# Two output banks taken in turn through the tail, and the second layer's weights loaded and cast every fifth slot

## The chip, the core and the metric

The kernel runs on one core of a Trainium2 chip. A core has five engines that run beside each other, each through its own instructions in order: TensorE (PE in the profile; its weight loads are listed as PEld), VectorE (DVE), ScalarE (ACT), GpSimd (POOL) and SyncE (SP), which here only issues DMA transfers. Engines wait for each other through semaphores. TensorE writes to PSUM, a memory of eight banks; VectorE and ScalarE read results from there and write them to SBUF, the working memory.

The metric is the device time of one execution in microseconds (us), shown as the median of several runs.

## The reference

An attention whose weights below a threshold are dropped, and then a two-layer network on its output. q, k and v have 8 batches of 8 heads, 576 rows and 64 columns; `x` has 4608 rows and 512 columns, `w_in` is 512 x 2048, `w_out` is 2048 x 512.

```python
scores = scale * np.matmul(q, k.transpose(0, 1, 3, 2))
thresh = np.max(scores, axis=-1, keepdims=True) - tau
scores = np.where(scores >= thresh, scores, -1000000000.0)
scores = scores - np.max(scores, axis=-1, keepdims=True)
attn = np.exp(scores)
attn = attn / (np.sum(attn, axis=-1, keepdims=True) + 1e-09)
attn_out = np.matmul(attn, v)
...
x = attn_out.transpose(0, 2, 1, 3).reshape(B * S, H * D)
h = x @ w_in
g = h - np.tanh(h)
out = g @ w_out
```

## The kernel before

**Attention.** Two heads form a pair (32 pairs, four to a batch), and a pair's 1152 rows of queries form nine tiles of 128, so there are 288 tiles. The main loop (line 681) has one slot `s` for each tile and some more on both ends. In slot `s` it issues the scores of tile `s + 8` (`scores`, lines 310 and 320, into two PSUM buffers `psS`), the thresholding of a tile some slots back (`kink`, line 367, ScalarE), the exp of tile `s` (`weights`) and the product with v of tile `s - 2` (`attend`, lines 422 and 433, into the PSUM tile `psO` of the pool `ps_o`, which has one buffer). `norm` (lines 447 to 453) takes `psO` out, and `emit_x` (lines 465 to 479) turns a pair's result and files it as `xT` and `xR`. VectorE takes each tile's scores out of PSUM with the row maximum (line 330).

**How z is turned.** For the first six pairs (tiles 0 to 53) TensorE transposes the thresholded tile z (line 387). From tile 54 on SyncE issues a DMA transpose for it (line 375), two tiles at a time or one alone, and ScalarE's exp of line 404 reads the result `zT`.

**Preparing a pair.** `plan` sets it out by tiles ahead of need. SyncE loads k, q and v (lines 149 to 157) some 14 to 16 tiles ahead into two buffers each. GpSimd splits k and q into a high and a low half (lines 183 to 187), later copies the turned k with its halves swapped (`kS`, line 263) and casts v (lines 215 to 220). For pair p, with r the tile whose scores the slot issues, the split of k stands at r = 9p - 8, the split of q at 9p - 7, the turn of k with its `kS` at 9p - 5, the cast of v at 9p - 4. The loads for it stand at 9p - 16 to 9p - 14.

**The weights.** `w_in` and `w_out` come in eight pieces each of 512 KB (128 x 1024 in f32). At every r in the list `w_when` (line 664) GpSimd casts the piece loaded at the event before (`w_cast`, line 618) and SyncE issues the load of the next (`w_load`, lines 626 and 630). The pool `wt` has two buffers, so a load waits for the cast of two pieces earlier. With the list of before the first eight events load `w_in`, the ninth (r = 35) casts the last piece of it and loads the first of `w_out`, and the seventeenth (r = 67) casts the last piece.

**The network.** It runs in nine blocks m: eight of 512 rows, one for each batch, and a ninth that gathers the 64 rows left over in each. `hidden` (line 488) makes one of sixteen columns of h from four matmuls of 512 columns; ScalarE's tanh (line 501, `bend`) and VectorE's subtraction (line 507, `shrink`) make g. `project` (line 514) makes a quarter of a group: for 128 rows (`ms` = 0 to 3) it adds four of the sixteen chunks of g times `w_out` into one PSUM tile `psY`; at the last quarter the tile is copied to the SBUF tile `yo` (lines 522 or 524; two buffers) and a store is put on SyncE's queue. A group is called (m, ms) below.

`layers(m, tail)` lists the steps of one stage: the sixteen `h_step` of block m, and between them the `y_step` of block m - 1 that are still to do, from its fourth quarter on. Stages 0 to 6 are spread over the slots of the attention (from slot 40 on), with the tail flag off. Stages 7 and 8 come after the last tile, with the flag on: first (6, 0)'s last quarter, (6, 1) to (6, 3), the first three quarters of (7, 0), then the rest of (7, 0), (7, 1) to (7, 3) and three groups of block 8. The last group is done in two halves of 256 columns (`y_half`).

**The banks of the tail.** `psY` comes from `ps_y`, which has one buffer. In the tail attention is done with `ps_o`, and a group may take that one; its copy is then made by ScalarE (line 522) and not by VectorE (line 524). Line 558 sets which: odd `ms` from block 7 on. So (6, 1), (6, 2), (6, 3) and (7, 0) follow each other on `ps_y`, and then (7, 1), (7, 3) and (8, 1) lie on `ps_o`. The first half of the last group takes `ps_o` and the second `ps_y`; ScalarE copies the first half, VectorE the second. In the tail h takes `psH` (two buffers) and `psHt` (the two buffers of the scores) in turn.

Of the kernel before, what the change touches and what calls it, by code (L numbers as in the profile page):

```python
# [18 lines left out]
def kernel(  # L19
# [14 lines left out]
    B, H, S, D = q.shape  # L34
# [96 lines left out]
    ps_o = pool("ps_o", 1, space=PSUM)  # L131
    ps_h = pool("ps_h", 2, space=PSUM)
    ps_y = pool("ps_y", 1, space=PSUM)
# [350 lines left out]
    def hidden(m, n, ps):  # L484
        if n == 0:
            gs[m] = g_pool.tile([P, DF_C, MB], BF16, name="g")
        for c in range(DM_C):
            nc.tensor.matmul(  # L488
                out=ps, lhsT=w_in_sb[:, c, n * P : (n + 1) * P],
                rhs=xs[m][:, c, :] if m < B else xR[:, c, :, :],  # L490
                start=(c == 0), stop=(c == DM_C - 1),
            )
        halves.append((m, n, ps))
# [18 lines left out]
    def project(m, ms, part, ps, last, cols=slice(0, d_model)):  # L512
        for n in range(4 * part, 4 * part + 4):
            nc.tensor.matmul(  # L514
                out=ps, lhsT=gs[m][:, n, ms * P : (ms + 1) * P],
                rhs=w_out_sb[:, n, cols], start=(n == 0), stop=(n == DF_C - 1),
            )
        if part == 3:
            nc_ = cols.stop - cols.start
            yo = y_pool.tile([P, nc_], F32, name="yo")  # L520
            if last:
                nc.scalar.copy(out=yo, in_=ps)
            else:
                nc.vector.tensor_copy(out=yo, in_=ps)  # L524
            if m < B:
                rows = out[m * S : m * S + MB, :].rearrange("(p c) n -> c p n", c=4)
                stores.append(lambda: nc.sync.dma_start(out=rows[ms], in_=yo))
            else:
                for h in range(2):
                    b = 2 * ms + h  # L530
                    eng = nc.scalar if h and nc_ < d_model else nc.sync
                    stores.append(
                        lambda b=b, h=h, eng=eng: eng.dma_start(
                            out=out[b * S + MB : (b + 1) * S, cols],
                            in_=yo[64 * h : 64 * h + 64, :],
                        )
                    )
# [8 lines left out]
    def layers(m, tail):  # L546


        def h_step(n):
            if tail and n % 2:  # L550
                ps = ps_big.tile([P, MB], F32, name="psHt", tag="big")
            else:
                ps = ps_h.tile([P, MB], F32, name="psH", tag="h")
            hidden(m, n, ps)

        def y_step(m, ms, part):
            if part == 0:
                odd = ms % 2
                odd = odd and m >= B - 1
                pl, tag = (ps_o, "o") if tail and odd else (ps_y, "y")  # L560
                ys[m, ms] = pl.tile([P, d_model], F32, name="psY", tag=tag), odd
            ps, odd = ys[m, ms]
            project(m, ms, part, ps, tail and odd)

        def y_half(h):

            n = d_model // 2
            pl, tag = ((ps_y, "y"), (ps_o, "o"))[1 - h]
            ps = pl.tile([P, n], F32, name="psY", tag=tag)
            for part in range(4):  # L570
                project(m, 3, part, ps, h == 0, slice(h * n, h * n + n))

        now = quarters(m - 1)[EARLY(m - 1) :] if m > 0 else []
        if m < NMB - 1:
            now += quarters(m)[: EARLY(m)]
        else:
            now += quarters(m)[:12]
        n = 16 + len(now)


        ahead = n - max(0, EARLY(m) - 3) - LAST if m < NMB - 1 else n - 9 - LAST
        steps, at, i = [], [], 0

        def ready(y):
            last = 4 * y[2] + 3
            return y[0] < m or len(at) > (last if m else 15) and at[last] + 2 < i

        while now or len(at) < 16:
            if len(at) < 16 and (
                not now or not ready(now[0]) or len(at) * ahead <= i * 16  # L590
            ) and not (m == B - 1 and i < FIRST):
                steps.append(lambda a=len(at): h_step(a))
                at.append(i)
            elif ready(now[0]):
                steps.append(lambda y=now.pop(0): y_step(*y))
            else:
                steps.append(lambda: None)
            i += 1
        if m == NMB - 1:
            steps += [lambda h=h: y_half(h) for h in range(2)]  # L600
        return steps
# [4 lines left out]
    def w_pieces():  # L606
        for w, sb, n in ((moe_w_in, w_in_sb, DM_C), (moe_w_out, w_out_sb, DF_C)):
            flat = sb.rearrange("p c n -> p (c n)")
            cols = n * w.shape[1] // 8
            src = w.rearrange("(c p) n -> p c n", p=P)  # L610
            for i in range(8):
                yield flat, src, i, cols, w.shape[1]
# [48 lines left out]
    for t in ("k", "q", "v"):  # L661
        load(1, t)
    pieces = w_pieces()
    w_when = [4 * i + 3 for i in range(17)]

    todo, stage = [], 0
    fold = const.tile([P, 64], BF16, name="fold")
# [122 lines left out]
```

## Time and profile before

| | |
|---|---|
| median of 7 runs | 539.14 us (538.36 to 540.0) |
| the profiled execution | 537.61 us |
| its span, first to last instruction | 535.8 us |
| granted TensorE clock | 0.999 |
| busy: TensorE, VectorE, ScalarE, GpSimd | 509.8, 428.1, 436.8, 290.1 us |
| first `psY` matmul | 113.1 us |
| last attention product (`psO`) | 465.2 us |
| first and last cast of `w_out` | 59.9 and 104.5 us |
| copies `yo`: VectorE, ScalarE | 33 and 4 |

The page divides the span into 40 slices and gives each engine's busy share of a slice in tenths. The groups say how often a line ran, how long one took, and what ended the engine's idle time before it. The chain of waits is followed back from the last instruction: each entry has its start, its length and the engine and line that worked; "issue" is time in which nothing that the profile shows was waited for. The timeline lists instructions with start and length, and in brackets the idle time of the engine just before. A DMA has the time at which it was issued and the time from there to its landing. The ends of matmuls are modelled.

### The profile page before, as it was taken

The numbers are of one execution on the slowest core, as the hardware profiler recorded it, in microseconds if no ns is written. First come the engines' busy times: TensorE is split into PE (matmuls) and PEld (weight loads), VectorE is DVE, ScalarE is ACT, GpSimd is POOL, SyncE is SP. The second block draws the span as 40 slices with busy tenths as digits, with TensorE's granted clock in tenths as the row PEclk, the third lists the DMA queues.
The fourth block names the chain that finished last, engine by engine and source line by source line (L and its number), as shares of the span: only waits on it lengthen the run. The fifth ranks groups of instructions, "written<-read, shape, count | busy, mean of one in ns | idle before, by whom it ended". The sixth has DMA issues, their size and how long they took to land.

```text
span 535.8 us, 13026 instructions
## 1 busy us (share of the span) xinstructions
PE 509.8 (95%) x4771; PEld 287.1 (54%) x4771; DVE 428.1 (80%) x1203; ACT 436.8 (82%) x628; POOL 290.1 (54%) x390
## 2 busy tenths in 40 slices
PE   5999899999999999999999999999999999999997
PEld 3666565555555555555555555555455555444444
DVE  5988888989888989888888988898888887554440
ACT  5999888999898989899888989898989989533330
POOL 7999996767555756666655755575666620000000
PEclk9999999999999999999999999999999999999999
DMA  7554657899988998899989899899989976300113
GB/s 215 170 185 150 206 177 145 187 189 180 197 178 160 183 206 182 168 174 188 197 175 198 182 195 189 161 176 203 186 164 175 204 135 116 88 30 30 39 41 78
DMA packets 204768, 85.76 MB, mean 160 GB/s; under 512 B 172320, under 2 KB 197152, under 8 KB 204704
## 3 DMA queue, kind: packets, MB, share of 16 engines
q1 hardware_dynamic: 204112, 84.51, 74.1%
q8 instruction: 37, 0.61, 0.5%
q10 hardware_dynamic: 592, 0.43, 0.3%
q14 instruction: 27, 0.22, 0.1%
HBM read 36.70 MB, written 9.44 MB: 86 GB/s over the span
## 4 chain that ended last, share of the span: by engine, by line
PE 70%; DVE 17%; ACT 4%; POOL 4%; issue 2%; DMA 1%; ACTq 0%; DVEq 0%; SPq 0%; POOLq 0%
PE psY L514 20%; PE psH L488 18%; PE psS L320 15%; DVE sc L330 8%; PE psO L433 5%; PE psS L310 3%; DVE g L507 3%; PE ps_k L234 3%; PE psHt L488 2%; ACT pT L396 2%; DVE kT L257 2%; DVE yo L524 2%; ACT z L367 1%; PE ps_q L234 1%; PE psZ L387 1%
## 5 line engine op out<-in xcount | busy, mean ns | idle before, releaser
L330 DVE TENSOR_SCALAR_CACHE_REDUCE sc<-psS 128x576 f32<-128x576 f32 x288 | 216.0, 752 | 23.3 <-PE psS L320 13.4
L367 ACT ACTIVATE z<-sc,nb 128x576 bf16<-128x576 f32 x256 | 193.4, 768 | 19.1 <-DVE nb L347 19.1
L514 PE MATMUL psY<-w_out_sb,g 128*128 128x512 bf16 (+1 forms) x592 | 146.0, 374 | 1.6 <-DVE yo L524 1.6
L263 POOL COPY kS<-kT 64x1152 f16<-64x1152 f16 x62 | 70.7, 1141 | 128.4 <-DVE nb L347 126.8
L404 ACT ACTIVATE pT<-zT 128x1152 f16<-128x1152 bf16 (+1 forms) x130 | 138.8, 1068 | 0.7 <-PE psX L471 0.5
L488 PE MATMUL psH<-xT,w_in_sb 128*128 128x512 bf16 x480 | 124.0, 379 | 2.3 <-DVE g L507 2.3
L320 PE MATMUL psS<-kT,qT 128*128 128x512 f16 (+1 forms) x512 | 104.9, 286 | 6.9 <-DVE sc L330 3.9
L501 ACT ACTIVATE th<-psH 128x512 f32<-128x512 f32 x128 | 75.4, 589 | 37.9 <-PE psH L488 36.7
L320 PEld LDWEIGHTS <-qT 128*128 128x128 f16 x1024 | 72.6, 97 | 56.5 <-issue 9.7
L507 DVE SCALAR_TENSOR_TENSOR g<-th,psH 128x512 bf16<-128x512 f32 x128 | 87.3, 682 | 18.9 <-ACT th L501 18.9
L320 PE MATMUL psS<-kS,qT 128*128 128x512 f16 x496 | 101.3, 286 | 0.3 <-POOL kS L263 0.3
L514 PEld LDWEIGHTS <-g 128*128 128x128 bf16 x592 | 50.7, 98 | 58.2 <-issue 5.7
L488 PEld LDWEIGHTS <-w_in_sb 128*128 128x128 bf16 x576 | 49.2, 98 | 58.2 <-issue 4.5
L433 PEld LDWEIGHTS <-pT 128*128 128x128 f16 x1280 | 55.7, 98 | 25.3 <-issue 1.9
L433 PE MATMUL psO<-vb,pT 128*128 128x65 bf16 x1280 | 61.2, 193 | 0.0
L187 POOL TENSOR_TENSOR qhl<-qraw,qhl 128x576 f16<-128x576 f32 x31 | 39.7, 1280 | 2.6
L187 POOL TENSOR_TENSOR khl<-kraw,khl 128x576 f16<-128x576 f32 x31 | 39.7, 1279 | 2.7
L396 ACT ACTIVATE pT<-psZ 128x640 f16<-128x640 bf16 (+1 forms) x54 | 35.4, 658 | 5.2 <-PE psZ L387 4.9
L257 DVE COPY kT<-ps_k 128x1152 f16<-128x1152 f16 x31 | 23.4, 756 | 13.8 <-PE ps_k L234 13.8
L524 DVE COPY yo<-psY 128x512 f32<-128x512 f32 (+1 forms) x33 | 22.5, 682 | 12.7 <-PE psY L514 7.6
L448 DVE TENSOR_TENSOR osb<-psO,rc 128x256 bf16<-128x256 f32 x64 | 27.2, 424 | 2.2
L234 PE MATMUL ps_k<-ident_f,khl 128*128 128x128 f16 x288 | 21.7, 220 | 5.3 <-DVE khl L200 5.2
(78 smaller groups left out, 504.9 us busy)
## 6 DMA issues: line engine op xcount, KB each, us to landing
vraw<-in_v_dram SPq DMA_DIRECT2D x32, 256.0 KB, 3.4
out_dram<-yo SPq DMA_DIRECT2D x32, 256.0 KB, 2.8
kraw<-in_k_dram SPq DMA_DIRECT2D x31, 256.0 KB, 3.2
qraw<-in_q_dram SPq DMA_DIRECT2D x31, 256.0 KB, 3.7
wt<-in_moe_w_in_dram SPq DMA_DIRECT2D x8, 512.0 KB, 4.6
wt<-in_moe_w_out_dram SPq DMA_DIRECT2D x8, 512.0 KB, 4.1
zT<-z SPq DMA_TRANSPOSE x104, 3.5
kraw<-in_k_dram SPq DMA_DIRECT2D x32, 32.0 KB, 3.0
```

The lines of the kernel that those rows point to most:

```text
L187: nc.gpsimd.tensor_tensor(out=hl[:, :, 1, :], in0=x, in1=hl[:, :, 0, :], op=ALU.subtract)
L263: nc.gpsimd.tensor_copy(out=o, in_=i)
L320: nc.tensor.matmul(out=ps[:, dst], lhsT=lhs, rhs=kk[:, src], start=(n == 0), stop=(n == 1),)
L330: nc.vector.tensor_scalar(out=sc, in0=ps[:, lo : lo + S], scalar1=SC, scalar2=None, op0=ALU.mult, op1=ALU.max, accum_out=mx[:, c : c + 1],)
L367: nc.scalar.activation(out=z, in_=sc, func=ACT.Prelu, bias=nb, scale=1.0, alpha=STEEP)
L396: nc.scalar.activation(out=pt[:, off * P : (off + n) * P], in_=ps[:, 0 : n * P], func=ACT.Exp)
L404: nc.scalar.activation(out=pt[:, 0 : n * P], in_=zts.pop(i)[:, 0:n, :], func=ACT.Exp)
L433: nc.tensor.matmul(out=po[:, (j - 1 - 5 * hh) + ab, :], lhsT=pt[:, blk * P : (blk + 1) * P], rhs=vb[:, hh, c, :], start=(n == 0), stop=(n ...
L488: nc.tensor.matmul(out=ps, lhsT=w_in_sb[:, c, n * P : (n + 1) * P], rhs=xs[m][:, c, :] if m < B else xR[:, c, :, :], start=(c == 0), stop= ...
L501: nc.scalar.activation(out=th, in_=ps, func=ACT.Tanh)
L507: nc.vector.scalar_tensor_tensor(out=gs[m][:, n, :], in0=th, scalar=-1.0, in1=ps, op0=ALU.mult, op1=ALU.add,)
L514: nc.tensor.matmul(out=ps, lhsT=gs[m][:, n, ms * P : (ms + 1) * P], rhs=w_out_sb[:, n, cols], start=(n == 0), stop=(n == DF_C - 1),)
```

## The change

The first two parts are in the tail. A group takes `ps_o` and ScalarE's copy if the tail flag is on, the group comes after (6, 1), and `ms` is even: (6, 2), (7, 0), (7, 2), (8, 0) and (8, 2). All others take `ps_y` and VectorE's copy. The halves of the last group exchange their banks: the first takes `ps_y`, the second `ps_o`; ScalarE still copies the first and VectorE the second.

The third part is the list of events for the weights. The first nine stay (r = 3, 7, ... 35). The other eight come at r = 40, 45, ... 75 and no longer at 39, 43, ... 67. An event both casts a piece and loads the next, so both move.

```diff
         def y_step(m, ms, part):
             if part == 0:
-                odd = ms % 2
-                odd = odd and m >= B - 1
-                pl, tag = (ps_o, "o") if tail and odd else (ps_y, "y")
+
+                odd = tail and (m, ms) > (B - 2, 1) and ms % 2 == 0
+                pl, tag = (ps_o, "o") if odd else (ps_y, "y")
                 ys[m, ms] = pl.tile([P, d_model], F32, name="psY", tag=tag), odd
             ps, odd = ys[m, ms]
-            project(m, ms, part, ps, tail and odd)
+            project(m, ms, part, ps, odd)
 
         def y_half(h):
 
             n = d_model // 2
-            pl, tag = ((ps_y, "y"), (ps_o, "o"))[1 - h]
+            pl, tag = ((ps_y, "y"), (ps_o, "o"))[h]
             ps = pl.tile([P, n], F32, name="psY", tag=tag)
             for part in range(4):
                 project(m, 3, part, ps, h == 0, slice(h * n, h * n + n))
...
     pieces = w_pieces()
-    w_when = [4 * i + 3 for i in range(17)]
+    w_when = [4 * i + 3 for i in range(9)] + [5 * i + 40 for i in range(8)]
```

## The prediction

> **What bounds the kernel now.** I read the page first (busy shares, slices), then the chain of waits cut to the tail and to its last microseconds, then the timeline of GpSimd and TensorE while the weights are cast, then the DMA issues one at a time where they share the queue with the transposes.
>
> ```profile
> PE 509.8 (95%) x4771; PEld 287.1 (54%) x4771; DVE 428.1 (80%) x1203; ACT 436.8 (82%) x628; POOL 290.1 (54%) x390
> POOL 7999996767555756666655755575666620000000
> ```
>
> TensorE is busy 95% of the span, but stage by stage the picture differs: GpSimd (POOL) is full in slices 2 to 6 (13 to 80 us) and idle after 440 us. The first part of the change sits where TensorE alone counts, the second just where POOL goes from full to half full. The granted clock is 0.999, so it plays no part.
>
> The tail, in the chain of waits (start, us, what):
>
> ```profile
> 470.86 0.88 PE psH L488 x4
> ...
> 472.42 0.57 issue
> 472.99 0.69 DVE yo L524
> 473.69 0.04 issue
> 473.73 1.02 PE psY L514 x4
> 474.75 0.86 PE psH L488 x4
> ...
> 501.54 0.86 PE psHt L488 x4
> 502.40 0.86 PE psY L514 x4
> 503.26 0.86 PE psH L488 x4
> ```
>
> The first six lines are a change of output tile on one PSUM bank: the next psY group can't begin until VectorE has copied the last one out. The last three are such a change with two banks (the ScalarE copy of (7, 1) starts at 501.57): 0.86 after 0.86, no gap. TensorE has no other gap from 466 us to its end, so what is saved there is saved at the end.
>
> The last transfer but one holds the last copy:
>
> ```profile
> 528.41 0.70 DVE yo L524
> 529.11 0.02 issue
> 529.13 0.47 SPq L533
> 529.60 0.05 issue
> 529.65 2.39 DMA out_dram<-yo
> ...
> 532.16 0.42 DVE yo L524
> ```
>
> The last half's copy waits for the buffer yo of (8, 2), whose store lands at 532.04; TensorE's last matmul ends at 531.86 (its merged row: 519.50 + 12.36).
>
> **The tail's banks, costed.** Before, (6,1), (6,2), (6,3) and (7,0) all take ps_y, and alternation begins at (7,1). After, (6,2), (7,0), (7,2), (8,0), (8,2) take ps_o with a ScalarE copy and the odd ones ps_y with VectorE, so three same-bank changes become alternating ones: (6,1) to (6,2), (6,2) to (6,3), (6,3) to (7,0). A step of four matmuls is 0.863 us without a stall (501.54 to 503.26 is two). From psH at 470.86 four steps end at 474.31; the trace has 474.75: 0.44. The same reading at 478.21 to 482.10 and 485.56 to 489.45 gives 0.44 each. **Sum: -1.31.** The change (6,0) to (6,1) stays on one bank (psY at 464.01, an idle of 0.78 before it), since ps_o still holds psO: VectorE reads it at 465.39. By 473.3, when (6,2) wants it, it has been free for some 7 us.
>
> Copies: ScalarE gains five of 0.585 us and loses three, VectorE the reverse at 0.69. They cost nothing, because ScalarE has 1.13 us idle before most tanh rows in the tail and was busy 6.57 of 20 us from 480 to 500; at 501.57 the copy stands directly ahead of a tanh (502.44, idle 0.28), and the matmul steps around it stay at 0.86. Without that cover each of the two added copies would push a tanh by 0.58: at most 1.2 us. The halves swap banks but still alternate: half 0 takes ps_y, left by (8,1) at 525.7 in old times, half 1 takes ps_o, left by (8,2) a full half (1.7 us) earlier. No wait is added. What is late next is the end: (8,2) is now copied in 0.585 instead of 0.69, so its store, and the last copy that waits for it, come 0.10 sooner (bounds 0 and 0.30, where the matmul itself would hold the copy). **Tail: -1.41.**
>
> **The weights' loads and casts, costed.** Nothing changes up to tile 35. The eight w_out pieces, with their loads (512 KB on SP's queue, issue 0.37 to 0.56 us) and casts (1.04 us on POOL), move: casts from tiles 39, 43, ... 67 to 40, 45, ... 75, loads from 35, 39, ... 63 to 35, 40, ... 70. The number of instructions is the same.
>
> On POOL:
>
> ```profile
> 59.87 1.04 POOL L618 CAST w_out_sb<-wt 128x1024 bf16<-128x1024 f32 x1
> 60.97 2.33 POOL L263 COPY kS<-kT 64x1152 f16<-64x1152 f16 x2
> ...
> 63.35 0.41 PE L320 MATMUL psS<-kS,qT 128*128 128x512 f16 x2 [0.29 <-POOL kS L263]
> ```
>
> The cast at 59.87 goes behind the copy kS, which starts at 59.93 (its source kT is there at 58.8), and TensorE's wait of 0.29 disappears. Nearly all of that is swallowed: the next VectorE row on the chain, sc at 63.91, waits for ScalarE's z (63.23 + 0.67), not for these matmuls, whose row ends at 63.76. I take -0.10, bounds 0 and -0.30. The later splits come at most 0.7 to 1.5 us sooner to consumers that don't wait for them (after 83 us POOL idles 2.8 to 5.9 us before every kS). The casts of tiles 70 and 75 fall at about 106 and 112 us into that idle time. First use of the last two pieces is the fourth quarter of (0,0) at about 125 us: cover 11 us. If the cover were gone, each would cost 1.04.
>
> The Trainium skill's page "SBUF — State Buffer", section "Who interferes with whom", speaks against shuffling POOL work under VectorE: an instruction that takes the shared port pair blocks the other engine for its whole length. The trace has 62 kS copies of 1139 to 1144 ns under a VectorE that is 80% busy, so nothing of it shows here; by the rule a moved copy could cost up to one VectorE row, 0.75, by the row 0.
>
> On SP's queue the loads at tiles 55 and later are passed by the transposes zT (issued from 84.86 on). Loads in that stretch: two before (87.74, 95.15), three after (about 90, 99.9 and 108). The one at tile 65 now stands behind the k load (98.68) and ahead of the q load and of this transpose:
>
> ```profile
> 101.20 1.78 SPq L375 DMA_TRANSPOSE zT<-z  x1
> zT<-z SPq DMA_TRANSPOSE x1, 5.5
> 107.61 1.15 ACT L404 ACTIVATE pT<-zT 128x1152 f16<-128x1152 bf16 x1
> ```
>
> (The second line, from the DMA view of 101 to 103 us, is its time to landing.) It lands at 106.7 and the exp takes it at 107.61: slack 0.9. A w load alone takes 3.9 us to land (issued at 76.89) and a 256 KB k load 3.0 (at 98.68), so 256 KB add 0.9 and 512 KB 1.8; less where the queue runs at its best. I take 1.6. The landing becomes 108.3 and ScalarE, gapless from 92 to 118 us, stands 0.7 longer. Behind it wait a tanh (110.00), for it VectorE's g (110.94, slack 0.36) and for that TensorE's psX (111.68): 0.3 of the 0.7 reach TensorE. I take +0.30. Lower bound 0 (the slack holds). Upper bound: the transpose issued at 88.49 right behind a load landed after 6.4, against 3.3 for an undisturbed one, so +3.1, less 0.9 of slack: +2.2. I am nearer the low end, because the k and q loads already delay this transpose (5.5 against 3.3) and the new load only lengthens that line. The load at about 108 is ahead of transposes with slack 3.5 and 3.8 us; removing the one at 87.74 helps rows that had slack 2.1 and 3.1. Both: 0.
>
> The page "DMA: Bandwidth & Descriptors", section "Queues, rings and completion order", says that each DMA engine takes the descriptors of one queue in ring order, which is the rule against putting a bulk load in front of transposes. At that page's 358 GB/s I estimate 1.5 us for 512 KB, and by it the exp would be 0.5 late instead of 0.7.
>
> **Sum.** -1.41 - 0.10 + 0.30 = -1.21. The profiled execution took 537.61 (span 535.8 and 1.81 around it), so 536.4 there. That execution is 1.53 below the median of the seven runs, 539.14 (538.36 to 540.0); a saving at the path's end carries over, so 539.14 - 1.21 = **537.9**, which is -0.22%. What a measurement can tell from no change is about 0.2%, 1.08 us: 538.06 and 540.22 are the marks.
>
> **Rivals.**
> 1. The slots' move is free or a gain: the exp is not late and the 0.29 counts in full. 539.14 - 1.41 - 0.30 = 537.4. For it: only 0.9 us of slack is attacked, by an uncertain queue. Against: ScalarE hides the 0.29. Chance 0.16.
> 2. The tail's gain is partly given back around 107 us: the whole 0.7 of the exp's lateness, or up to twice that, reaches TensorE, undamped, since from 111.68 on TensorE is on the chain. 539.14 - 1.41 + 0.7 = 538.4, with + 1.4 539.1. For it: ScalarE is gapless there. Against: g has slack. Chance 0.20.
> 3. Slower: SP's queue becomes the bound. One mechanism: a load directly ahead of a transpose costs 3.1, as at 88.49, and this happens at the loads of tiles 65 and 70. The first gives 3.1 - 0.9 = 2.2; the second is still unabsorbed at the transposes issued at 114.09 (landed 118.34, used 119.87, slack 1.5), which gives 1.6. 3.8 - 1.41 = +2.4: 541.5. It decides from a total loss of 2.5 us. For it: the transpose issued at 118.61 lands at 122.76 and ScalarE takes it at 122.86 after an idle of 0.51, so slack does reach zero. Against: the DMA digits show empty slices between. Chance 0.12.
> 4. The banks alternate but the wait only changes its name: the copy on ScalarE queues behind a tanh and psY waits as long for it. Tail about 0, total 539.3. The rows at 501.57 and 515.39 speak against it. Chance 0.05.
>
> **Chances.** The forecast has 0.47, with its own range 537.5 to 538.3 (0.39 of it below 538.06). Faster: 0.39 + 0.16 = 0.55. Same: 0.08 + 0.20 + 0.05 = 0.33. Slower 0.12. The range 537.2 to 539.6 takes in rivals 1, 2 and 4 and most of the unknown cost's upper bound (539.14 - 1.41 + 2.2 = 539.9); it leaves out rival 3 and the last of that bound.
>
> **What the new profile would show.** ScalarE's copies yo six (five full ones), VectorE's 31; no psY group behind a VectorE yo wait but the one near 464; steps of 0.86 from there to the end. kS of the fifth pair at about 59.9 and no POOL wait at 63. The sixth transposed exp, near 107.6: its idle time is the price of part two. If the distance from the first psY (113.1) to the old 470.00 psY has changed, something I hold to be steady is not. I am wrong if the start of layer two's first psY moves by more than 1 us, or if the tail from 464 on shortens by less than 1.

## The result, and the profile after

The changed kernel takes 540.43 us (median of 13 runs, 539.35 to 541.29) against 539.14 (median of 31 runs of the kernel before, 538.12 to 541.00). The ratio is 1.0024 with an interval of 1.0015 to 1.0033: slower by 0.24%, 1.29 us. The forecast was 537.9 in a range of 537.2 to 539.6. Its profiled execution took 540.67 us, with a span of 538.9.

First, of the kernel after, the busy time of each engine and the granted clock from the page, and two groups from the lines view (busy, mean ns of one, idle time of the engine before them and what ended it).

```profile
PE 510.5 (95%) x4771; PEld 287.9 (53%) x4771; DVE 427.3 (79%) x1201; ACT 438.0 (81%) x630; POOL 290.7 (54%) x390
...
PEclk9999999998999999999999999999999999999999
...
L514 PE MATMUL psY<-w_out_sb,g 128*128 128x512 bf16 (+1 forms) x592 | 146.0, 374 | 0.8 <-DVE yo L524 0.8
...
L524 DVE COPY yo<-psY 128x512 f32<-128x512 f32 (+1 forms) x31 | 21.1, 682 | 13.4 <-DMA out_dram<-yo 6.5 <-PE psY L514 4.9
```

VectorE made 31 copies and ScalarE six, and only one wait of psY for VectorE's copy is left, 0.8 us. The clock row has a dip in the tenth slice (121 to 135 us) that the kernel before did not have; the busy shares hide everything else.

**The tail** did what it was to do. The chain of waits of the kernel after, from the first step on (start, us, what):

```profile
470.85 0.90 PE psH L488 x4
...
473.47 0.86 PE psHt L488 x4
474.34 0.86 PE psY L514 x4
475.20 0.86 PE psH L488 x4
```

No step is longer than the others, and no copy yo stands between them. From the start of the last attention product to the end of the span it is 69.37 us, against 70.67: 1.30 less. Its last microseconds in the same chain:

```profile
531.47 0.59 ACT yo L522
...
532.60 2.37 DMA out_dram<-yo
534.97 0.03 issue
535.00 0.05 DVEq L524
...
535.10 0.05 DVEq L524
...
535.19 0.42 DVE yo L524
```

The store lands 3.50 us after ScalarE's copy began, where it was 3.63 behind VectorE's. But VectorE's queue now shows two waits before the last copy, not one, and they take 0.10 back.

**The copy kS** is ahead of the cast. GpSimd's timeline after (start, us, what):

```profile
61.28 2.32 POOL L263 COPY kS<-kT 64x1152 f16<-64x1152 f16 x2
63.67 1.04 POOL L618 CAST w_out_sb<-wt 128x1024 bf16<-128x1024 f32 x1
```

TensorE's wait for it (0.29 us before, at 63.35) is gone. Against the first profile of the kernel before, the VectorE row `sc` of a tile (line 330) starts 1.35 us later at tile 44 and 1.06 later at tile 48: 0.29 gained in that stretch.

**What was lost** lies between 118 and 127 us. The chain of waits there:

```profile
102.06 7.12 DMA zT<-z
109.17 0.02 issue
109.19 1.10 ACT pT L404
...
117.25 0.35 POOL kS L263
117.60 0.77 issue
118.37 4.89 DMA qT<-qhl
123.26 0.05 issue
123.31 1.14 PE psS L320 x4
```

Two transfers are on it. The first is the transpose that the forecast spoke of: 7.12 us to landing where it was 5.5, and the exp waits 0.4 for it. The second is the DMA transpose of pair 9's q (line 246), on which tile 81 and the eight that follow depend. Before, it landed in 3.45 us, at 119.28. TensorE's timeline of the kernel before, at the scores of tile 80 and then of tile 81 (two instructions each, with kT and with kS):

```profile
118.92 0.41 PE L320 MATMUL psS<-kT,qT 128*128 128x512 f16 x2
119.16 0.41 PE L320 MATMUL psS<-kS,qT 128*128 128x512 f16 x2
119.40 0.41 PE L320 MATMUL psS<-kT,qT 128*128 128x512 f16 x2
```

and of the kernel after (in brackets the idle time and what ended it):

```profile
120.18 0.41 PE L320 MATMUL psS<-kT,qT 128*128 128x512 f16 x2
120.43 0.41 PE L320 MATMUL psS<-kS,qT 128*128 128x512 f16 x2
123.31 0.66 PE L320 MATMUL psS<-kT,qT 128*128 128x512 f16 x2 [2.47 <-DMA qT<-qhl]
```

So it had 0.12 us to spare. (The next scores, at 120.52, are those of tile 82: VectorE's `sc` of tile 81 starts at 120.60, before they end.) ScalarE waits too, in the waits of 100 to 132 us (engine and line, what for, us in total, times, longest):

```profile
ACT pT L404 <- DMA zT<-z: 2.0, 2, 1.6
```

And the stretches around it in the windows view (length; busy us and count of instructions of TensorE, its weight loads, VectorE, ScalarE and GpSimd; granted clock, DMA share, GB/s):

```profile
122.00:123.30 1.30, 0.00 (x0) 0.00 (x0) 0.00 (x0) 1.30 (x3) 1.21 (x2) 0.98 0.63 168
123.30:125.00 1.70, 1.69 (x15) 1.09 (x16) 0.42 (x1) 0.32 (x1) 1.64 (x3) 0.50 1.21 271
125.00:127.00 2.00, 2.00 (x19) 0.95 (x17) 1.74 (x8) 1.16 (x1) 1.33 (x2) 0.59 0.75 141
```

TensorE stands still, and then works at half clock: the clock's own record has 0.5 from 123.24 for 3.41 us. The lateness of `sc` against the kernel before jumps from 1.27 at tile 80 to 3.98 at tile 81, and creeps to 4.5 by tile 85, while the clock is halved: 3.2 us. That is where the tail's gain went, and more. It is not this one execution alone: the mean granted clock of the span was 0.995 to 0.997 in all 13 runs of the changed kernel, and 0.998 to 1.000 in each of the 102 runs of the kernel before that were made beside the experiments below. Of the thirteen profiles, the four with a stretch of half clock behind such a stall have 0.995 to 0.997 by that figure, and the nine without have 0.998 or more.

### The profile page after: what moved, and what is told of

Same layout as the page of the kernel before. It is cut to its first block, busy times and chain, and to the rows that moved or that the text cites. A ratio compares the mean times of both kernels' runs of the same rounds, so it can differ in the third digit from the quotient of the medians.

```text
span 538.9 us, 13027 instructions
## 1 busy us (share of the span) xinstructions
PE 510.5 (95%) x4771; PEld 287.9 (53%) x4771; DVE 427.3 (79%) x1201; ACT 438.0 (81%) x630; POOL 290.7 (54%) x390
## 4 chain that ended last, share of the span: by engine, by line
PE 73%; DVE 11%; ACT 8%; DMA 4%; issue 2%; POOL 0%; SPq 0%; DVEq 0%; ACTq 0%
PE psY L514 21%; PE psH L488 18%; PE psS L320 16%; PE psO L433 5%; DVE sc L330 5%; ACT pT L396 3%; PE psS L310 3%; ACT z L367 3%; PE psHt L488 3%; PE ps_k L234 2%; DVE g L507 2%; DMA qT<-qhl 2%; PE psZ L387 1%; DMA zT<-z 1%; DVE yo L524 1%
## 5 line engine op out<-in xcount | busy, mean ns | idle before, releaser
L524 DVE COPY yo<-psY 128x512 f32<-128x512 f32 (+1 forms) x31 | 21.1, 682 | 13.4 <-DMA out_dram<-yo 6.5
```

## The experiments

Each kernel is compared with runs of the kernel before on the same chip (medians there 538.97 to 539.28). "Lateness" is again the start of a tile's `sc` against the first profile of the kernel before. The theory, A in the expectations: SyncE's queue runs late behind the moved loads, and TensorE stands at pair 9's q for it. The rivals are named with each run.

**One part alone.** `tail_only` is the changed kernel with the old list of events, `slots_only` the kernel before with the new list:

```diff
-    w_when = [4 * i + 3 for i in range(9)] + [5 * i + 40 for i in range(8)]
+    w_when = [4 * i + 3 for i in range(17)]
```

(for `slots_only` the other way round, with the old tail.)

> The tail's banks alone, the weights' events as before. Theory A (the w_out loads push the DMA transpose of pair 9's q late, TensorE stalls 2.5 us on it and its clock is halved for 3.4 us after): that stall is absent, the first 470 us are those of before, and the tail's gain stands alone: 539.14 - 1.3 = 537.8 (537.3 to 538.3). Rival B (the time is lost in the tail, where a wait only changes its name): 539.1 to 540.4.

> The weights' events as in the changed kernel, the tail's banks as before. Theory A: the stall on pair 9's q near 121 us and the halved clock are there, and the three same-bank waits of the tail too: 540.43 + 1.3 = 541.7 (541.2 to 542.3). Rival B: 539.1, since nothing of the slots' move costs. Rival C (the changed kernel's later start of 1.4 us in its profile is part of the change): 540.5.

`tail_only`: 538.54 us, ratio 0.9992 [0.9981, 1.0003]; TensorE has no wait of over 0.3 for qT, the clock is whole, and from the last attention product to the end it is 69.36. `slots_only`: 542.83, ratio 1.0064 [1.0043, 1.0085]; TensorE waits 3.1 for qT, half clock for 3.4 us from 124.3, and the end is 70.66 after the last product, as before. So the loss belongs to the list of events and the 1.30 to the tail. In time the tail alone brings about 0.5, less than the trace's 1.3; the interval reaches from a gain of 1.0 us to none. `slots_only` is 2.4 above the changed kernel, of which the tail explains 1.3; with six runs its interval is wide enough for that.

**The stall taken away.** `q9_on_pe` turns pair 9's q on TensorE, as every second pair's is; SyncE's queue loses one transpose.

```diff
-        return p >= 2 * HPAIR and (p % 2 == 1 or p == 30)
+        return p >= 2 * HPAIR and p != 9 and (p % 2 == 1 or p == 30)
```

> The changed kernel, but pair 9's q is turned by TensorE and copied by VectorE, as pair 8's is, and no DMA transpose is issued for it. Theory A: the stall of 2.5 us and the halved clock go; nine more transposes (0.5 us) and a copy of 0.75 us come: 540.43 - 3.2 + 0.6 = 537.8 (537.3 to 538.6). Rival D (the price is paid by ScalarE, which waits 0.4 and 1.6 us for the transposes of z): the waits stay, 539.8 to 540.4.

538.61, ratio 0.999 [0.9979, 1.0001]; the stall and the half clock are gone, the lateness grows by 1.1 at tiles 76 to 80 and by nothing at 84 to 88. It is 1.8 less than the changed kernel: the stall's price is real. It doesn't say why the transpose is late.

**The clock kept up.** `keep_busy` puts six matmuls whose result nobody reads into the gap before the scores of tile 81, so that TensorE is not idle for as long.

```diff
         if 0 <= s + AHEAD - 1 < NTILE:
             shift(s + AHEAD - 1)
+        if s + AHEAD == 9 * TPP:
+            pd = ps_h.tile([P, MB], F32, name="psD", tag="h")
+            for c in range(6):
+                nc.tensor.matmul(
+                    out=pd, lhsT=w_in_sb[:, 0, 0:P], rhs=w_in_sb[:, 0, 0:MB],
+                    start=True, stop=True,
+                )
```

> The changed kernel with six extra matmuls of 512 columns (1.3 us), whose result nobody reads, just ahead of the scores of tile 81, where TensorE waits for pair 9's q. Theory A with the clock: the idle stretch falls from 2.5 to some 1.2 us, the clock stays whole, the 1.7 us that the half clock cost come back: 538.7 (538.3 to 539.4). Rival E (the stall alone is the price, the clock costs nothing that later slack doesn't absorb): 540.4, or 541.7 if the extra matmuls are in the way.

540.29, ratio 1.0023 [1.0009, 1.0037]: as slow as the changed kernel. Its timeline has the same late transpose, and a shorter idle:

```profile
123.59 0.42 PE L320 MATMUL psS<-kT,qT 128*128 128x512 f16 x2 [1.45 <-DMA qT<-qhl]
```

The granted clock stays 1.00 in every window behind it (and its mean is 0.998 or more in eleven of the twelve runs), and in the profile tiles 80 to 88 lose 2.5 and not 3.2, about the size of the stall alone. In the times nothing is left of these 0.7 us. What the halved clock costs is shown in the profile and not resolved in the times; the expectation of 538.7 was wrong.

**The transpose ahead of its need.** `qT_earlier` issues pair 9's q transpose one tile sooner.

```diff
-        d = 5 if q_by_dma(p) else 3 - (p == 1)
+        d = 5 + (p == 9) if q_by_dma(p) else 3 - (p == 1)
```

> The changed kernel with one move on SP's queue: pair 9's transposing DMA of q is issued one tile earlier, ahead of the loads of pair 10's q and of one transpose of z; nothing else differs. Theory A (this transfer's lateness is the loss): it lands about 2 us sooner, TensorE's stall on it falls from 2.5 to under 1 us, the clock stays whole: 540.43 - 2.5 = 537.9 (537.4 to 538.8). Rival D (the transposes of z, which now stand one place further back, are the price): ScalarE waits longer for them, 540.4 to 541.5.

539.81, ratio 1.001 [0.9997, 1.0023]. qT lands 3.51 us after its issue and TensorE doesn't wait for it, but a transpose of z issued at 118.06 lands at 122.85, 4.80 later, ScalarE has stood idle for 2.2 when the exp takes it at 122.96, and the lateness grows by 1.8 between tiles 80 and 88 (1.0 in the second profile of the kernel before, below). Part of the loss goes on under a new name: the line of transfers is late, not this one transfer alone. The profiled execution, 538.25 us, is the fastest of the twelve, so it shows the mild case; three others have a mean clock of 0.996 and take 540.85 to 541.46.

**The loads out of SyncE's queue, at the same slots.** `loads_on_act` issues the last three loads of `w_out` (events 60, 65 and 70) from ScalarE's queue. Bytes and slots stay; the time of issue does not, as the trace shows: 89.66, 96.68 and 104.68 us, where the changed kernel has 90.96, 100.31 and 109.38.

```diff
-            nc.sync.dma_start(out=wt.rearrange("p (c n) -> p c n", n=width), in_=s)
+            eng = nc.scalar if i >= 5 else nc.sync
+            eng.dma_start(out=wt.rearrange("p (c n) -> p c n", n=width), in_=s)
```

> The changed kernel with the last three loads of w_out issued from ScalarE's queue in place of SP's, at the same slots. If it is the place in SP's queue that delays the transposes behind them (theory A1): pair 9's q lands as early as in the kernel before, no stall, 537.9 (537.4 to 538.8). If it is the bytes on the shared DMA engines (theory A2): the transfer still lands late and the time stays at 540.4 (539.6 to 541.2).

537.63, ratio 0.9974 [0.9963, 0.9986]: faster than the kernel before, 2.8 below the changed one. The DMA view of this kernel has, for 117 to 118 us and then for 104 to 105 us (median us from issue to landing at the end):

```profile
qT<-qhl SPq DMA_TRANSPOSE x1, 3.4
...
wt<-in_moe_w_out_dram ACTq DMA_DIRECT2D x1, 512.0 KB, 7.1
zT<-z SPq DMA_TRANSPOSE x1, 8.2
```

The transpose of q is on time: TensorE's idle time for it is 0.2. The load takes 7.1 us, where the three took 4.4 to 5.2 in the changed kernel. The bytes are not free here either: the transpose of z issued just ahead of it, at 103.95, takes 8.2 us to land, longer than the slowest in the changed kernel (7.1), and the exp waits 1.1 for it; 0.4 of that is left in the lateness at tile 80. So these three loads, as SyncE issued them at the new slots, are the cause of the stall. Which part of it went with the place in the queue and which with the earlier issue is not told apart: no run issued all three from SyncE at these times. (`load15_earlier`, below, comes as early with the last one alone, at 105.12 from SyncE, and keeps the stall.)

**Which of the loads?** `load15_earlier` moves the last one away (event 70 to 67), `one_load_on_act` puts only the load of tile 65 on ScalarE's queue.

```diff
-    w_when = [4 * i + 3 for i in range(9)] + [5 * i + 40 for i in range(8)]
+    w_when = [4 * i + 3 for i in range(9)] + [40, 45, 50, 55, 60, 65, 67, 75]
```

```diff
-            eng = nc.scalar if i >= 5 else nc.sync
+            eng = nc.scalar if i == 6 else nc.sync
```

(the second against `loads_on_act`.)

> The changed kernel with only the event of tile 70 moved to tile 67: the last load and the cast of the piece before. Theory A with the last load as the cause: it is through some 4 us before pair 9's q, the stall of 2.5 us falls below 1, no halved clock: 538.0 (537.5 to 539.0). If the load at tile 65 and the line behind it are the cause: the stall stays, 540.4, and the wait of ScalarE near 109 us grows from 0.4 to above 1.

> The changed kernel, with only the load of tile 65 (the one behind the k load, at about 100 us) issued from ScalarE's queue; the loads of tiles 60 and 70 stay on SP's. Theory L (this one load starts the delay that carries on to pair 9's q transpose): that transpose lands within 3.6 us of its issue, TensorE waits less than 0.5 us for it, no stretch at half clock, time 537.9 (537.2 to 538.6). Rival M (the load of tile 70 at about 109 us, the last one before it, is as much to blame): the wait for qT stays above 1.5 us and the time at 540.0 or more. Rival N (all three loads in SP's queue share in it): the wait shrinks to between 0.5 and 1.5 us, and the time lies between 538.6 and 540.0.

`load15_earlier`: 541.07, ratio 1.0029 [1.0015, 1.0043]; the wait of 2.5 and the half clock stay. `one_load_on_act`: 539.61, ratio 1.0007 [0.9994, 1.002]; its runs go from 537.78 to 540.85, and the profiled one, 540.36, has the stall:

```profile
122.90 0.42 PE L320 MATMUL psS<-kT,qT 128*128 128x512 f16 x2 [2.37 <-DMA qT<-qhl]
```

The granted clocks of the single runs tell them apart: in `one_load_on_act` eight of twelve have 0.995 to 0.997 and a median of 540.26, four have 1.000 and a median of 538.42; in `load15_earlier` seven of nine have 0.995 to 0.997. So neither the load of tile 65 nor the slot of the load of tile 70 is the cause alone, and changing one of them spares TensorE the half clock in some executions only. The load of tile 60 was not tried by itself.

**Versions without the loss.** `tail_and_kS_first` has the new tail and a list that keeps the cast behind the copy kS but brings the late loads forward to where they were. `all_combined` has that list and the last four loads on ScalarE's queue.

```diff
-    w_when = [4 * i + 3 for i in range(9)] + [5 * i + 40 for i in range(8)]
+    w_when = [4 * i + 3 for i in range(9)] + [40, 43, 49, 51, 55, 59, 63, 67]
```

> The tail's banks as changed, and of the slots' move only the part that lets GpSimd copy kS ahead of a cast: events at tiles 40, 43, 49, 51, 55, 59, 63, 67 instead of 39, 43, 47, 51, ...; the loads that fall among the transposes stay where the kernel before has them. Theory A: no stall on pair 9's q, the tail's 1.3 and the 0.3 of kS are kept: 539.1 - 1.6 = 537.5 (537.0 to 538.5). If kS brings nothing: as the tail alone, 538.5 measured.

> The changed kernel's tail, the eight events at 40, 43, 49, 51, 55, 59, 63 and 67, and the last four loads of w_out issued from ScalarE's queue. Theory A1 (the place in SP's queue is what costs, and the rest of the change gains): the gains add, 1.3 in the tail and 0.29 at the copy kS, and nothing is paid near 120 us: 537.4 (536.8 to 538.0). Rival H (what remains is the hole in the data queue near 121 us, which falls on one transpose or another wherever the loads are): no better than the two versions before it, 537.6 to 538.6, with a late transpose of z of 1 us or more left between tiles 84 and 88.

`tail_and_kS_first`: 538.3, ratio 0.9972 [0.996, 0.9983]; qT lands in 3.30 us, the 0.29 at kS and the 1.30 in the tail are both there. `all_combined`: 538.33, ratio 0.9991 [0.9981, 1.0001]: no better, the gains don't add. Tiles 53 to 56 lose 1.3 us that no other kernel loses; GpSimd and ScalarE there, from the chain and from ScalarE's timeline:

```profile
74.39 1.04 POOL w_out_sb L618
75.43 0.02 issue
75.46 0.39 ACTq L627
```

```profile
73.08 0.59 ACT L396 ACTIVATE pT<-psZ 128x512 f16<-128x512 bf16 x1
75.46 0.39 ACTq L627 DMA_DIRECT2D wt<-in_moe_w_out_dram  x1
75.89 0.77 ACT L367 ACTIVATE zm<-sc,nb 128x576 bf16<-128x576 f32 x1 [2.23 <-DVE nb L347]
```

The load needs the buffer that GpSimd's cast is to free, and now it is ScalarE that stands in line for it: idle from 73.67 to 75.46. (The view names VectorE's `nb` for the wait.) In `loads_on_act` the buffers are free when the three loads come up, and ScalarE pays 0.4 us for each issue, beside its own running work.

**The kernel before, once more.** `before_again` is unchanged.

> The kernel before, unchanged, for a second profile of it: how far one execution's profile stands for the kernel. Theory V (the late start of the first k load and the late transpose near tile 84 to 88 differ from execution to execution): the start offset of the first scores is not the first profile's but up to 2 us later, the transposes of z near 121 us may wait 1 us or more, and the time is 539.1 (538.6 to 539.7), ratio 1.000. Rival P (both belong to the changed kernels): the first scores begin within 0.2 us of the first profile's time, and there is no wait above 0.6 us near tile 84 to 88.

539.43, ratio 1.0009 [0.9999, 1.0019]. Its profiled execution took 539.85 us (the first 537.61, below all 31 runs of its set). Its first scores begin 0.8 later than in the first profile, because a part of the first k lands 0.7 later, and by tile 2 it is 1.55 late; then it loses 1.0 at tiles 84 to 88, where the exp waits 1.5 for a transpose of z. Both had looked like effects of the change and are not. In this profile the span is 538.1, so that the changed kernel's is 0.8 longer, not 3.0.

## Why the prediction was wrong, by its steps

**The three stalls, -1.31: right.** All three are gone, every step is 0.86, the stall at (6,0) to (6,1) stays at 0.8, and ten profiles with the new tail have 69.31 to 69.39 us from the last product to the end, against 70.66 to 70.67 in the three with the old one. The copies cost nothing, and rival 4 is out.

**The -0.10 at the end: not there.** The store did land sooner, measured from the copy; a second wait on VectorE's sequencer takes the same 0.10. What released it isn't shown. The tail is -1.30 in the span and not -1.41.

**The copy kS, -0.10: too small.** 0.29 came through, the bound; it is seen in every profile with the new order (1.35 to 1.06, and in `tail_and_kS_first` 1.18 to 0.89), and 0.10 of it in the second profile of the kernel before too, which leaves about 0.2 for the change.

**The transpose near 107, +0.30: right for what it covered.** It landed in 7.12 and not in 5.5, which is the 1.6 that the forecast took; the exp waited 0.42 (forecast 0.7), and 0.21 reached the tiles.

**"The load at about 108 is ahead of transposes with slack 3.5 and 3.8 us ... Both: 0": this step failed.** It was put at nothing after a look at the transposes of z alone; the transpose of pair 9's q stands on the same queue, and TensorE stood still 2.47 us for it. SyncE's timeline before and then after, from the transpose of `zm` to that of q:

```profile
106.64 1.27 SPq L375 DMA_TRANSPOSE zT<-zm  x1
108.01 3.40 SPq L375 DMA_TRANSPOSE zT<-z  x2
111.50 0.55 SPq L149 DMA_DIRECT2D kraw<-in_k_dram  x1
...
115.83 1.29 SPq L246 DMA_TRANSPOSE qT<-qhl  x1
```

```profile
107.13 2.15 SPq L375 DMA_TRANSPOSE zT<-zm  x1
109.38 0.54 SPq L626 DMA_DIRECT2D wt<-in_moe_w_out_dram  x1
110.01 3.87 SPq L375 DMA_TRANSPOSE zT<-z  x2
113.94 0.57 SPq L149 DMA_DIRECT2D kraw<-in_k_dram  x1
...
118.37 1.30 SPq L246 DMA_TRANSPOSE qT<-qhl  x1
```

The transpose of `zm` takes 2.15 to issue where it took 1.27 (1.22 in the second profile of the kernel before), the load adds 0.54, and the pair of transposes behind it takes 0.47 more, which need not be the load's doing: in that second profile, with no load there, the pair takes 3.90. The transpose of q is issued 2.54 later than before, 1.06 of which the whole kernel was late before this stretch: 1.48 of delay. Its time to landing is 4.89 and not 3.45, 1.44 more. Less the 0.12 of slack, and the 0.21 that the tiles were late already from the exp at 109, that makes 2.6, and tile 81 lost 2.7. The other 0.5 came with the halved clock. In the second profile of the kernel before there is no slack to take off: q lands at 120.72, and its scores begin at 120.77. The forecast had no term for this transfer, the one that TensorE itself reads. Nor is its delay the work of this one load, as `one_load_on_act` and `load15_earlier` show.

**Of the rivals** the third was nearest: it named SyncE's queue and the loads of tiles 65 and 70, and its total was 541.5. It put the price on the transposes of z; `qT_earlier` shows that this one can take the price over, but in the changed kernel it falls on qT. Nobody had the clock in the sum. The profile from which the slacks were read was better than usual as well: near 123 us the exp waited 0.51 for a transpose of z, and 1.5 near 125 us in the second profile. The forecast's sign of being wrong, a first psY more than 1 us away, did come up (114.39 against 113.12), but not for the change: in the second profile of the kernel before it is at 114.33.

**What the sum should have been.** Against the second profile of the kernel before: the tail -1.30, kS -0.19, and from tile 48 to tile 88 the changed kernel loses 3.44 (1.06 to 4.50) where that one loses 1.03 (1.21 to 2.24), +2.41. Together +0.9; the spans differ by 0.8, the medians by 1.29.

The Trainium skill's page "TensorE: Matmul & The Clock Gate", section "The HAM clock gate", says that the gate falls to half rate after about one window of 3.4 us without work and needs one such window of work to rise again. The return agrees, 3.41 us here. The fall came after idle times of 2.47, 2.46, 3.09 and 2.37 us, all shorter than that window, and did not come after 1.45.

Its page "DMA: Bandwidth & Descriptors", section "Issuing engines are not separate DMA queues", says that transfers issued from several engines share the same 16 DMA engines, and that spreading the issues saves the sequencer's time only, which is usually small. Here three loads moved to another engine made 2.8 us of 540.43, with the same bytes. How much of that is sequencer time saved on SyncE, how much the place in its queue and how much the earlier issue of the loads is not told apart.

**Open.** Why the tail alone gives about 0.5 us in the times (interval of the ratio 0.9981 to 1.0003) and 1.30 in every trace; what the halved clock costs in the times; whether the loads' place in SyncE's queue or their later issue delays the transpose; and the cause of the hole described below.

## What to carry to other kernels

When a bulk load changes its slot, list every transfer on its queue until the queue is empty again, the ones that TensorE reads itself above all, with the slack of each counted to the instruction that truly reads it (here 0.12 us in one profile and none in the other; one row further on it looked like 1.24), and add up issue times as well as landing times. A load whose buffer is free for certain can go to another engine's queue, away from transposes with little slack, though a transpose in flight beside it may still land late (8.2 us here); where it must still wait for its buffer, that engine stands with it. And a second profile of the kernel before is worth its run: the first here was 1.5 us under the median, which made 2 us of usual loss look like the change's.

## What the runs showed of the hardware

**A hole in the data queue.** Near 121 us, in most of the profiles, SyncE's queue moves next to nothing for 0.75 to 1.75 us with transfers in flight. In `before_again` (windows view, columns as above, DMA share and GB/s last):

```profile
120.00:121.00 1.00, 1.00 (x16) 0.47 (x13) 0.50 (x3) 1.00 (x2) 0.85 (x4) 1.00 0.87 237
...
121.50:122.50 1.00, 0.88 (x12) 0.47 (x9) 0.96 (x6) 1.00 (x2) 0.85 (x3) 1.00 0.05 7
...
123.00:124.00 1.00, 1.00 (x20) 0.71 (x17) 0.96 (x5) 0.57 (x1) 1.00 (x2) 1.00 1.15 213
```

Twelve of the thirteen profiles have one, and in each of them a fetch of instructions (8 KB, then 16 KB, on queues of their own) stands ahead of it, the 16 KB begun 0.3 to 1.7 us earlier. Where the transpose of q had landed by then, it took 3.3 to 3.7 us; where it was still in flight, 4.5 to 5.0. The exception is `one_load_on_act`: its q took 4.99 with the same fetch at 120.82, and the queue runs low only from 122.65, 0.2 us before the landing. That the fetch causes the hole, or the hole the added time, was not tried.

**The clock.** An idle time of TensorE of 2.4 to 3.1 us was followed by half clock for 3.4 us, and one of 1.45 was not. In `one_load_on_act` the halving began at 124.1, 1.2 us after TensorE had gone back to work.

**The start.** The first scores begin up to 1.4 us, and the first tiles up to 2.2 us, later than in the first profile, in kernels whose code up to there is the same.
